# Attention over inducing points, then a gated layer: the first batch's prologue rewritten, and the hidden units dealt out in another order

## The chip, the cores and the metric

One core of a Trainium2 chip runs the whole program. Its engines work side by side and are tied by semaphores: TensorE (PE in the profile, its weight loads PEld), VectorE (DVE), ScalarE (ACT), GpSimd (POOL) and SyncE (SP), which here only issues DMAs. The metric is the device time of one execution in microseconds; a smaller one is better.

## The reference, cut to what matters

```python
# x: (4, 12416, 128), inducing: (32, 128); w_gate, w_val: (128, 1536), w_out: (1536, 128)
def mab(q, kv):                                   # scale = 1/sqrt(128)
    s = scale * (q @ kv.transpose(0, 2, 1))
    s = s - s.max(-1, keepdims=True)
    a = np.exp(s)
    a /= a.sum(-1, keepdims=True) + 1e-09
    return a @ kv
h = mab(I, x)                                     # 32 inducing rows attend over all 12416 rows
y = mab(x, h)                                     # each row attends over the 32 rows of h
gate = 1 / (1 + np.exp(-(y @ w_gate)))
return gate * (y @ w_val) @ w_out
```

So a batch's `h` needs every row of that batch before the first row of output can be made. The kernel never forms `y`: it multiplies `h` into the two weight matrices once per batch (`hw`, 32 rows by 2 x 1536 columns) and applies the attention weights `a2` to that.

## The kernel before, in words

**Groups and stages.** A batch is 97 chunks of 128 rows: six groups of 16 chunks and one odd chunk. *Stage 1* (`s1_...`) takes a group's scores against the inducing rows, their maximum per 32-partition strip, the exponentials, and the weighted sum of the rows. *Combine* rescales the seven group sums to one maximum, adds them and gives `hT` (`h_take`). `hw_fill` multiplies `hT` into the weights: four matmuls per half, two from `wg16` and two from `wv16`, each of 32 x 384 outputs into its own strip of 32 partitions; a ScalarE copy brings the half into the tile `hwt`. *Stage 2* (`s2_...`) gives each chunk's weights `a2` over the 32 rows of `h`, four times side by side (`s2_spread`), transposed so that they can be multiplied with `hwt`.

**The main loop.** 97 blocks of four chunks go through 12 slices of 128 hidden units each, taken two and one at a time: `steps`, 776 of them. For step t, `hidden_mm` makes the gate (`g_ps`) and the value (`v_ps`) from `hwt` and `a2`; `gate` is ScalarE's tanh of the gate (sigmoid by tanh, line 830); `product` is VectorE's `(t + 1) * v` into `u` (line 841); `project` multiplies `u` with `wo16` into `acc_ps` (line 870), which ScalarE copies out once per block. The gate fill of step t + 2 follows the value fill of step t, so TensorE's order is value t, gate t + 2, then whatever else is planned there, then projections.

**What sets the order.** The schedule is written by hand: every engine runs its instructions in the order of the Python calls. `plan` maps a slot (two steps, about 1.7 us apart) to the pieces of the next batch's stage 1, combine and stage 2 that are issued there; `part` (an `hw_fill` half) and `keep` (its copy) are such pieces, two of each for each of three later batches. A wait in front of an instruction holds everything behind it on the same engine.

**The prologue** (batch 0) has no main loop to hide behind. POOL's queue issues the loads: batch 0's six groups, the last in two pieces of 12 and 4 chunks, then the three weight matrices and the first three groups of batch 1. As each group lands, TensorE transposes it (`x_turn`, line 631, into `xt_ps`), VectorE copies the first eight chunks to `xT` and ScalarE the rest. The first three groups in order of arrival (`EARLY` = 3) are combined on GpSimd while later ones still come. For the rest the chain at the end is: maximum of the last group, `ml` over all columns, weights `wl`, four scaled sums added by VectorE; beside it GpSimd and ScalarE find the common maximum over the four strips (`join_min`, lines 352 to 367), whose factor `w4` scales `e32l` and `e32w`; two matmuls (lines 735 and 737) give the sum of weights and `h`. After `hT` the first block of four chunks (`a2n_a`, `a2T`, `a2first`) is done by VectorE and TensorE, the other twelve chunks through two DMA transposes on SP.

**Dummy matmuls.** `keep_on(n, tag)` issues n matmuls of 128 x 512 that nobody reads. Their operand `idle` is the last four chunks of `xT[0]`, so a real copy into those four chunks has to wait until the dummies issued before it have read them.

Of the kernel before, what the change touches and what calls it, by code (L numbers as in the profile page):

```python
# [19 lines left out]
BC = 4  # L20
# [5 lines left out]
def kernel(  # L26
# [73 lines left out]
    def keep_on(n, tag):  # L100
# [33 lines left out]
        wo16[:].rearrange("p j c -> p (j c)"), moe_w_out.rearrange("(p j) c -> p (j c)", j=NJ)  # L134
    )
    for g in range(3):
        x_load(1, g)
# [24 lines left out]
    EARLY = NS - 4  # L162
# [115 lines left out]
    def s1_sum_keep(b, s, hp):  # L278
        ng, w, R = s1_dims(s)
        width = C + 1 if b else C  # L280
        summed[b] += 1
        if b == 0 and at_col[s] > EARLY:
            return hp[:, 0:C]
        nc.scalar.copy(out=hsts[b % 2][0:R, at_col[s], 0:width], in_=hp[0:R, 0:width])
# [51 lines left out]
    def hw_fill(b, hf, tag):  # L336
        hw_ps = ps.tile([P, NI // 2, P], F32, tag=tag, name="hw_ps")
        for r in range(4):
            wsrc = wg16 if r < 2 else wv16
            nc.tensor.matmul(  # L340
                hw_ps[32 * r : 32 * r + 32, :, :],
                hT16[b][:],
                wsrc[:].rearrange("c (f i t) -> c i t f", i=NI, t=2)[:, ts(hf, NI // 2), r % 2, :],
# [3 lines left out]
        return hw_ps  # L347

# [21 lines left out]
    def plan_combine(b, lead, weights, fill):  # L370
# [45 lines left out]
        def keep(hf):  # L416
            if hf == 0:
                st["hwt"] = bp.tile([P, NI, P], F16, tag="hw", bufs=B, name="hwt")
            nc.scalar.copy(out=st["hwt"][:, ts(hf, NI // 2), :], in_=st["hw_ps"][:])  # L419
            if hf == 1:  # L420
                hw[b] = st["hwt"]
# [218 lines left out]
    for p in range(-2, NS - 3):  # L640
# [7 lines left out]
        if p >= 0:  # L648
            s = arrival[p]
            a1[s] = s1_turn_copy(s, s1_turn_pe(0, s, a1T[s]))  # L650
# [3 lines left out]
        if p + 1 == EARLY - 1:  # L654

# [7 lines left out]
            lw = const.tile([P, EARLY], F32, tag="lwe")  # L663
            nc.gpsimd.tensor_tensor(out=lw[:], in0=l1[:, 0:EARLY], in1=we[:], op=ALU.mult)
            add_tree(lw, EARLY, l1l[:, 0:1])
# [12 lines left out]
        elif p == EARLY - 1:  # L678
            pool_part(1)
        elif p == EARLY:  # L680
            pool_part(2)
# [7 lines left out]
    s = arrival[EARLY]  # L689
    s1_sum(0, s, a1[s], "acc")  # L690
    a1T[sb] = s1_exp(0, sb, s1)
    aT = s1_turn_pe(0, sa, a1T[sa])
    a1T[sc] = s1_exp(0, sc, s1_score(0, sc, "g1"))
    keep_on(4, "acc")


    ml = const.tile([P, 1], F32, tag="ml")
    nc.vector.tensor_reduce(out=ml[:], in_=nml[:], axis=AX.X, op=ALU.min)
    wl = const.tile([P, 1 + NS - EARLY], F32, tag="wl")
    nc.scalar.activation(out=wl[:], in_=nml[:], func=AF.Exp, bias=ml[:], scale=-1.0)  # L700
    nc.scalar.mul(out=hpart[0][:], in_=hpart[0][:], mul=wl[:, 0:1])
    a1[sa] = s1_turn_copy(sa, aT)
    a1[sb] = s1_turn_copy(sb, s1_turn_pe(0, sb, a1T[sb], "g2"))
    hps = [hst[:, EARLY, 0:C], s1_sum(0, sa, a1[sa], "acc")]
    lw = const.tile([P, 1 + NS - EARLY], F32, tag="lwl")
    nc.vector.tensor_mul(out=lw[:], in0=l1l[:], in1=wl[:])
    lsum = const.tile([P, 1], F32, tag="lsum0")
    nc.vector.reduce_sum(out=lsum[:], in_=lw[:], axis=AX.X)
    e32s = const.tile([P, m], F32, tag="e32s")
    nc.scalar.mul(out=e32s[:], in_=e32[:], mul=lsum[:])  # L710
    top = join_min(const, ml, (1, 3))
    w4 = const.tile([P, 1], F32, tag="w4")
    nc.scalar.activation(out=w4[:], in_=ml[:], func=AF.Exp, bias=top[:], scale=-1.0)
    e32l = const.tile([P, m], F32, tag="e32l0")
    nc.scalar.activation(
        out=e32l[:], in_=e32s[:], func=AF.Identity, bias=tiny[:], scale=w4[:]
    )
    e32w = const.tile([P, m], F32, tag="e32w")
    nc.scalar.mul(out=e32w[:], in_=e32[:], mul=w4[:])

    a1[sc] = s1_turn_copy(sc, s1_turn_pe(0, sc, a1T[sc], "v2"))
    hps.append(s1_sum(0, sb, a1[sb], "m"))
    hps.append(s1_sum(0, sc, a1[sc], "v1"))
    keep_on(4, "g2")
    for k, hp in enumerate(hps):
        nc.vector.scalar_tensor_tensor(
            out=hpart[0][:],
            in0=hp,
            scalar=wl[:, 1 + k : 2 + k],
            in1=hpart[0][:],  # L730
            op0=ALU.mult,
            op1=ALU.add,
        )
    l_ps = ps.tile([P, m], F32, tag="g1", name="l_ps")
    nc.tensor.matmul(l_ps[:], ones[:], e32l[:], start=True, stop=True)
    h_ps = ps.tile([P, m], F32, tag="m", name="h_ps")
    nc.tensor.matmul(h_ps[:], hpart[0][:], e32w[:], start=True, stop=True)
    keep_on(2, "g2")
# [19 lines left out]
    s2_score(0, NLO + BC, 0, GC - BC, s2_b)  # L758
    hl_b = s2_max(GC - BC, s2_b)
    hw[0] = bp.tile([P, NI, P], F16, tag="hw", bufs=B, name="hwt")  # L760
    hw_ps = [hw_fill(0, 0, "g1"), hw_fill(0, 1, "v1")]
    keep_on(2, "g2")
    for hf in range(2):
        nc.scalar.copy(out=hw[0][:, ts(hf, NI // 2), :], in_=hw_ps[hf][:])
# [5 lines left out]
    e_b = s2_exp(GC - BC, s2_b, *hl_b)  # L770
    a2T = ps.tile([P, BC, P], F16, tag="m", name="a2T_ps")
    for j in range(BC):
        nc.tensor.transpose(
            a2T[:, j, :],
            a2n_a[2 * j // BC][:, j % (BC // 2), :, :].rearrange("p r k -> p (r k)"),
            ident[:],
        )
    a2first = s2p.tile([P, BC, P], F16, tag="a2first", bufs=1)
    keep_on(1, "g2")
    nc.vector.tensor_copy(out=a2first[:], in_=a2T[:])  # L780
# [203 lines left out]
```

## Time and profile before

| | us |
|---|---|
| Median of three runs (lowest, highest) | 729.85 (728.44, 729.98) |
| The profiled execution's own time | 727.66 |
| Its span, first to last instruction | 725.8 |
| Busy in that span: VectorE, ScalarE, TensorE, GpSimd | 706.7, 676.7, 648.4, 419.4 |
| Start of the first product (line 841) in the span | 32.26 |

The profiled execution is one of the same program under the hardware profiler; 1.9 us of its time lie outside the span. Lines of the timeline read: start, duration, engine, line, operation, out<-in, how many are merged (`x4`), and in brackets the idle time before it and who ended it. Lines of the windows read: stretch, its length, busy time of the engine and in brackets its number of instructions, granted TensorE clock, share of the DMA engines, GB/s.

### The profile page before, as it was taken

The page shows a single profiled execution, that of the slowest core. Times are in us where ns is not written, and L with a number is a line of the kernel's source. Part 1 is how long each engine was busy: PE and PEld are TensorE (multiplying, and loading weights), DVE is VectorE, ACT ScalarE, POOL GpSimd, SP SyncE. Part 2 cuts the span into 40 slices and gives each one's busy share as a digit, 9 for nine tenths or more (in the row PEclk, how much of TensorE's full clock was granted, in tenths as well). Part 3 has the DMA queues.
Part 4 walks back from the last instruction along what each step waited for, and adds up shares of the span by engine and source line. Part 5 has one row for each costly group of instructions (what it writes and reads, how often), then busy time and mean ns, then how long its engine had stood idle before and what let it go on. Part 6 is the DMA issues. An engine that isn't in the chain of part 4 may idle for free.

```text
span 725.8 us, 21496 instructions
## 1 busy us (share of the span) xinstructions
PE 648.4 (89%) x8437; PEld 390.4 (54%) x8437; DVE 706.7 (97%) x874; ACT 676.7 (93%) x1011; POOL 419.4 (58%) x702
## 2 busy tenths in 40 slices
PE   7888899999998998999989988999899899898887
PEld 4455555555555555555555555555555555555555
DVE  4899999999999999999999999999999999999998
ACT  4799999999999999999999999999999999999996
POOL 4463754887654648488666266387755665636200
PEclk9999999999999999999999999999999999999999
DMA  9999635242459253235248431220223122131311
GB/s 173 174 188 159 126 81 117 63 101 72 92 117 170 73 113 87 62 79 114 59 119 160 104 75 53 67 75 30 76 59 67 52 60 71 46 62 45 61 45 46
DMA packets 116342, 65.21 MB, mean 90 GB/s; under 512 B 99824, under 2 KB 100496, under 8 KB 116240
## 3 DMA queue, kind: packets, MB, share of 16 engines
q1 hardware_dynamic: 111936, 49.81, 30.1%
q0 software_dynamic: 4032, 13.90, 10.7%
q8 instruction: 66, 1.08, 0.6%
q14 instruction: 36, 0.29, 0.1%
q10 hardware_dynamic: 272, 0.13, 0.1%
HBM read 27.80 MB, written 25.43 MB: 73 GB/s over the span
## 4 chain that ended last, share of the span: by engine, by line
DVE 50%; issue 21%; PE 17%; ACT 9%; DMA 2%; DVEq 1%; POOL 0%; ACTq 0%; POOLq 0%
DVE u L841 47%; ACT t L830 8%; PE acc_ps L870 8%; PE v_ps L812 6%; DMA xn<-in_x_dram 2%; DVE nm L221 2%; PE hw_ps L340 1%; DVEq L841 1%; ACT a1T L234 1%; PE g_ps L812 0%; PE hp_ps L269 0%; POOL xn L81 0%; ACT hwt L419 0%; PE w_ps L103 0%; PE s_ps L437 0%
## 5 line engine op out<-in xcount | busy, mean ns | idle before, releaser
L841 DVE SCALAR_TENSOR_TENSOR u<-t,v_ps 128x1024 f16<-128x1024 f16 (+1 forms) x777 | 675.6, 944 | 3.1 <-PE g_ps L812 2.9
L830 ACT ACTIVATE t<-g_ps 128x1024 f16<-128x1024 f32 (+1 forms) x776 | 594.0, 818 | 28.7 <-ACT t L830 17.3
L812 PE MATMUL v_ps<-a2r,hwt 32*128 32x512 f16 (+1 forms) x1188 | 292.4, 371 | 65.9 <-DVE u L841 64.2
L870 PE MATMUL acc_ps<-wo,u 128*128 128x128 f16 x4656 | 327.3, 220 | 1.0
L870 PEld LDWEIGHTS <-u 128*128 128x128 f16 x4656 | 261.6, 98 | 89.3 <-issue 87.4
L812 PE MATMUL g_ps<-a2r,hwt 32*128 32x512 f16 (+1 forms) x1188 | 295.4, 377 | 0.0
L812 PEld LDWEIGHTS <-hwt 32*128 32x128 f16 x2400 | 90.5, 91 | 199.4 <-issue 153.3
L506 POOL TENSOR_TENSOR sum<-e 128x256 f32<-128x256 f16 (+1 forms) x23 | 15.5, 672 | 144.5 <-ACT e L498 142.5
L552 POOL TENSOR_TENSOR a2n<-e,rs 128x2048 f16<-128x2048 f16 (+2 forms) x24 | 86.3, 3594 | 6.8 <-DVE rs L524 5.1
L530 POOL TENSOR_TENSOR near<-sme,minus 128x16 f32<-128x16 f32 (+1 forms) x22 | 65.2, 2966 | 1.8
L888 ACT ACTIVATE o<-acc_ps 128x512 f32<-128x512 f32 x96 | 58.0, 605 | 0.9
L485 POOL TENSOR_SCALAR rise<-rise 128x256 f32<-128x256 f32 (+6 forms) x110 | 51.2, 466 | 9.7
L484 POOL TENSOR_TENSOR rise<-sc 128x256 f32<-128x256 f32 (+1 forms) x22 | 16.3, 739 | 40.1 <-ACT sc L474 39.8
L486 POOL TENSOR_TENSOR top<-top,rise 128x128 f32<-128x128 f32 (+3 forms) x88 | 28.4, 323 | 7.3
L506 POOL TENSOR_TENSOR sum<-sum 128x128 f32<-128x128 f32 (+3 forms) x92 | 28.4, 309 | 7.2
L484 POOL TENSOR_TENSOR rise<-top 128x128 f32<-128x128 f32 (+3 forms) x88 | 27.3, 311 | 6.9
L489 POOL TENSOR_TENSOR sc<-sc,top 128x512 f32<-128x512 f32 (+1 forms) x22 | 23.9, 1086 | 1.7
L437 PEld LDWEIGHTS <-xT 128*128 128x128 f16 x388 | 13.1, 96 | 11.8 <-issue 11.7
L81 POOL DMA_DIRECT2D xn<-in_x_dram x25 | 14.7, 596 | 6.6 <-DMA xn<-in_x_dram 5.7
L437 PE MATMUL s_ps<-hT,xT 128*128 128x32 f16 x388 | 18.1, 178 | 0.1
L486 POOL TENSOR_TENSOR top<-sc,rise 128x256 f32<-128x256 f32 (+1 forms) x22 | 16.2, 738 | 1.8
L234 ACT ACTIVATE a1T<-s_ps,nm 128x512 f16<-128x512 f32 (+1 forms) x24 | 15.0, 626 | 1.7 <-DVE nm L221 1.7
(121 smaller groups left out, 245.1 us busy)
## 6 DMA issues: line engine op xcount, KB each, us to landing
out_dram<-o SPq DMA_DIRECT2D x96, 256.0 KB, 2.1
xn<-in_x_dram POOLq DMA_DIRECT2D x19, 512.0 KB, 7.2
xn<-in_x_dram POOLq DMA_DIRECT2D x4, 544.0 KB, 5.9
a2r<-a2n SPq DMA_TRANSPOSE x29, 4.4
xn<-in_x_dram POOLq DMA_DIRECT2D x1, 384.0 KB, 14.7
wg<-in_moe_w_gate_dram POOLq DMA_DIRECT2D x1, 384.0 KB, 16.2
wv<-in_moe_w_val_dram POOLq DMA_DIRECT2D x1, 384.0 KB, 16.4
wo<-in_moe_w_out_dram POOLq DMA_DIRECT2D x1, 384.0 KB, 15.7
```

The lines of the kernel that those rows point to most:

```text
L437: nc.tensor.matmul(s2[:, j, :], xT[b][:, c + j, :], hT16[b][:], start=(j == 0), stop=whole and j == j1 - 1, skip_group_check=True,)
L484: nc.gpsimd.tensor_tensor(out=r, in0=far, in1=near, op=ALU.subtract)
L485: nc.gpsimd.tensor_scalar_max(out=r, in0=r, scalar1=0.0)
L486: nc.gpsimd.tensor_tensor(out=top[:, 0:n, 0:w], in0=near, in1=r, op=ALU.add)
L506: nc.gpsimd.tensor_tensor(out=d[:, 0:n, :], in0=src[:, :, 0:w], in1=src[:, :, w : 2 * w], op=ALU.add)
L530: nc.gpsimd.tensor_tensor(out=near[:, 0:n], in0=sme[:, 0:n], in1=minus1[:, 0:n], op=ALU.pow)
L552: eng.tensor_tensor(out=a2n[:, 0:n, :, :], in0=e.unsqueeze(2).to_broadcast((P, n, 4, m)), in1=rs.unsqueeze(2).unsqueeze(3).to_broadcast((P ...
L812: st[what + "end"] = nc.tensor.matmul(pt[:, k, col : col + nb * P], hw[b][r : r + 32, j // 2, :], a2r[r : r + 32, o : o + nb, :].rearrange ...
L830: st["tanh"] = nc.scalar.activation(out=st["t"][:], in_=st["g"][:], func=AF.Tanh, scale=0.5)
L841: u = nc.vector.scalar_tensor_tensor(out=st["u"][:, :, c:e], in0=st["t"][:, :, c:e], scalar=1.0, in1=st["v"][:, :, c:e], op0=ALU.add, op1= ...
L870: nc.tensor.matmul(acc[0][(i // 2) % len(acc[0])][:, i, :], st["u"][:, k, ts(i, P)], wo16[:, j, :], start=(j == 0 and i in ((0, 2) if len( ...
L888: nc.scalar.mul(out=o32[:], in_=acc[0][0][:], mul=0.5)
```

## The change

The hidden units are dealt out in another order. Before, slice j = 2i + t of `hwt` took the columns f * 12 + j of the weights, so a fill read every twelfth column; now a fill reads 384 columns that lie side by side, and the copy out of PSUM (`hw_take`) picks every third value instead. `wo16` is loaded in the matching order, in four pieces per partition instead of one.

In the prologue: `EARLY` is 4; the sum of the fourth group is finished behind the loop; the last group's transposes are split 8, 4 and 4, with the copy of the middle four on ScalarE; the maximum over the four strips is found by TensorE (`mlT_ps`: `ml` turned into a row; a reduction; four small matmuls that subtract it into `arg_ps`), so that one exponential gives the final `wl`; the four scaled sums are added by TensorE in PSUM; `join_min` is no longer called for batch 0. The first block's weights are not spread: 16 transposes write the four strips. The other twelve chunks' `a2n_b` goes from VectorE to GpSimd and behind the first half of the first product (`turn_b`). The first step's gate fill, tanh and product are cut in halves. Batch 1's third group is loaded later, and some of batch 1's slots move by one to three.

```diff
-        wo16[:].rearrange("p j c -> p (j c)"), moe_w_out.rearrange("(p j) c -> p (j c)", j=NJ)
+        wo16[:].rearrange("p (q i) c -> p q (i c)", i=NI // 2),
+        moe_w_out.rearrange("(q p i) c -> p q (i c)", p=P, i=NI // 2),
...
-    EARLY = NS - 4
+    EARLY = NS - 3
...
     def hw_fill(b, hf, tag):
...
-                wsrc[:].rearrange("c (f i t) -> c i t f", i=NI, t=2)[:, ts(hf, NI // 2), r % 2, :],
+                wsrc[:, ts(2 * (r % 2) + hf, F // 4)],
...
+    def hw_take(hwt, hf, hw_ps):
+        nc.scalar.copy(
+            out=hwt[:, ts(hf, NI // 2), :], in_=hw_ps[:].rearrange("r (f i) -> r i f", i=NI // 2)
+        )
...
-    x_turn(0, c0, GC - BC, "g2")
     s1 = s1_score_pe(0, sb, "v1")
-    x_turn(0, c0 + GC - BC, BC, "v2")
     s1_max(0, sb, s1)
...
+    x_turn(0, c0, GC // 2, "g2")
+    xt = ps.tile([P, 2, 8, P], F16, tag="v2", name="xt_ps")
+    for j in range(GC // 2):
+        nc.tensor.transpose(xt[:, j // BC, j % BC, :], xn[0][:, c0 + GC // 2 + j, :], ident[:])
+        if j == BC - 1:
+            two = nc.scalar.copy(
+                out=xT[0][:, c0 + GC // 2 : c0 + n - BC, :], in_=xt[:, 0, 0:BC, :]
+            )
+    keep_on(2, "acc")
+    one = nc.vector.tensor_copy(out=xT[0][:, c0 + n - BC : c0 + n, :], in_=xt[:, 1, 0:BC, :])
...
+    nc.tensor.matmul(mlT_ps, ml[:], identf[:], start=True, stop=True)
+    nc.tensor.matmul(arg_ps, identf[:], nml[:], start=True, stop=True, skip_group_check=True)
...
+    for g in range(4):
+        nc.tensor.matmul(
+            low_ps[32 * g : 32 * g + 32, 1, 0:NL],
+            top[:],
+            ones[0:1, 0:NL],
...
+    nc.scalar.activation(out=wl[:], in_=arg_ps, func=AF.Exp, scale=-1.0)
...
+    nc.gpsimd.tensor_tensor(out=lw[:], in0=l1l[:], in1=wl[:], op=ALU.mult)
+    add_tree(lw, NL)
...
-    top = join_min(const, ml, (1, 3))
...
+        nc.tensor.matmul(h_ps[:], hw_parts[k], e32[:], start=(k == 0), stop=(k == NL - 1))
...
-    a2n_a = [
-        s2_spread(BC // 2, e_a[:, j : j + BC // 2, :], rs_a[:, j : j + BC // 2], nc.vector)
-        for j in range(0, BC, BC // 2)
-    ]
...
     for j in range(BC):
...
+        for r in range(4):
+            nc.tensor.transpose(a2T[32 * r : 32 * r + 32, j, :], a2n_a[:, j, :], ident[:])
...
+            cuts = [0, 512] if t else [0, 256, 512]
...
+            if t == 0 and c == 0:
+                turn_b()
...
-            [(11, (18, 19, 19)), (16, (23, 23, 23))]
+            [(13, (18, 19, 19)), (16, (23, 23, 23))]
...
-            when = 3 * g if b else (7, 10, 13, 16, 19, 22, 11)[g]
+            when = 3 * g if b else (9, 11, 14, 17, 20, 23, 12)[g]
```

Where instructions move: three places. Rows name line, operation, out<-in, shape, and in brackets the engines or DMA queues (DMASW) whose semaphores are waited for.

TensorE, at the last group's transposes (`xt_ps`), the dummies (`w_ps`) and the last group's scores (`s_ps`). Before:

```order
L209 MATMUL s_ps<-xT_87,indT 32x512 [waits Activation_49]
L209 MATMUL s_ps<-xT_87,indT 32x512
...
L631 MATMUL xt_ps<-ident,xn_92 128x128 [waits PE_49]
...
L269 MATMUL hp_ps<-xn_92,a_358 32x128 [waits Activation_49]
...
L209 MATMUL s_ps<-xT_87,indT 32x512 [waits DVE_49]
...
L103 MATMUL w_ps<-xT_87 128x512 [waits Activation_49]
```

Now:

```order
L637 LDWEIGHTS xn_92 [waits DMASW5_49]
...
L695 MATMUL xt_ps<-ident,xn_92 128x128 [waits PE_49]
...
L695 LDWEIGHTS xn_92 [waits DMASW6_49]
L695 MATMUL xt_ps<-ident,xn_92 128x128 [waits Activation_49]
...
L103 MATMUL w_ps<-xT_87 128x512 [waits PE_49]
...
L210 MATMUL s_ps<-xT_87,indT 32x512 [waits DVE_49]
...
L270 LDWEIGHTS a_409 [waits DVE_49]
```

The last four transposes now wait for ScalarE, whose copy reads the same PSUM tile; two dummies follow them, and the copy of the last four chunks on VectorE (line 701) stands behind those dummies. The weighted sum of the fourth group (`a_409`) has moved behind the last scores.

GpSimd, between the early groups' sums (`hpart`) and stage 2 of the first group (`hi`). Before:

```order
L673 TENSOR_TENSOR hpart_284<-hpart_284,hpart_285 128x128 [waits Pool_49]
L352 COPY quad<-ml 32x1 [waits DVE_49]
L352 COPY quad<-ml 32x1 [waits Pool_49]
...
L353 TENSOR_SCALAR quad<-quad 32x1 [waits Pool_49]
L361 TENSOR_SCALAR quad<-quad 32x1 [waits Pool_49]
L367 COPY top<-quad 32x1 [waits Pool_49]
...
L452 CAST hi<-nmx 128x12 [waits DVE_49,Pool_49]
```

Now:

```order
L680 TENSOR_TENSOR hpart_320<-hpart_320,hpart_321 128x128 [waits Pool_49]
L748 TENSOR_TENSOR lw<-l1l,wl 128x4 [waits Activation_49]
L325 TENSOR_TENSOR lw<-lw 128x2 [waits Pool_49]
L325 TENSOR_TENSOR lw<-lw 128x1 [waits Pool_49]
L751 TENSOR_SCALAR e32l<-e_124,lw 128x32 [waits Pool_49]
L458 CAST hi<-nmx 128x12 [waits DVE_49]
```

`join_min` is gone; in its place stand four operations that start only when ScalarE has made `wl`, each waiting for the one before, and `e32l` is what the sum of weights (`l_ps`) needs.

TensorE, at the first step. Before:

```order
L812 MATMUL g_ps<-a2first,hwt 128x512 [waits PE_49]
L812 MATMUL g_ps<-a2first,hwt 128x512
...
L812 MATMUL v_ps<-a2first,hwt 128x512
...
L103 MATMUL w_ps<-xT_87 128x512 [waits Activation_49]
```

Now:

```order
L103 MATMUL w_ps<-xT_87 128x512 [waits PE_49]
...
L853 MATMUL g_ps<-a2first,hwt 128x256 [waits PE_49]
...
L853 MATMUL g_ps<-a2first,hwt 128x256
...
L853 MATMUL g_ps<-a2first,hwt 128x256 [waits DVE_49]
...
L853 MATMUL g_ps<-a2first,hwt 128x512
...
L853 MATMUL v_ps<-a2first,hwt 128x512
```

The two gate matmuls of step 0 have become four half ones, the second pair waiting for VectorE's second half of `a2first`. The first tanh half waits for the fourth of them, not the second; the second tanh half has no wait of its own.

More of the change, by code (lines that the diff above doesn't have):

```diff
@@ L418, in keep @@
                 st["hwt"] = bp.tile([P, NI, P], F16, tag="hw", bufs=B, name="hwt")
[L419 removed]
+            hw_take(st["hwt"], hf, st["hw_ps"])
             if hf == 1:
@@ L690 @@
+    keep_on(2, "acc")
+    one = nc.vector.tensor_copy(out=xT[0][:, c0 + n - BC : c0 + n, :], in_=xt[:, 1, 0:BC, :])
+    tc.declare_no_dep(one.ins, two.ins, reason="each reads a bank of its own")
+    a1T[sb] = s1_exp(0, sb, s1)
+    s = arrival[EARLY - 1]
+    a1[s] = s1_turn_copy(s, aT)
+    s1 = s1_score_pe(0, sc, "g1")
+    s1_max(0, sc, s1)
     s1_sum(0, s, a1[s], "acc")
-    a1T[sb] = s1_exp(0, sb, s1)
-    aT = s1_turn_pe(0, sa, a1T[sa])
-    a1T[sc] = s1_exp(0, sc, s1_score(0, sc, "g1"))
@@ new lines @@
+    a1[sb] = s1_turn_copy(sb, aT)
+    hps = [s1_sum(0, sa, a1[sa], "acc")]
+    for g in range(4):
[3 more added lines that the diff above has]
+            ones[0:1, 0:NL],
+            start=False,
+            stop=True,
+            skip_group_check=True,
+        )
+    aT = s1_turn_pe(0, sc, a1T[sc], "v1")
+    wl = const.tile([P, NL], F32, tag="wl")
+    nc.scalar.activation(out=wl[:], in_=arg_ps, func=AF.Exp, scale=-1.0)
+    hw_parts = [hpart[0][:]] + [hst[:, NS - k, 0:C] for k in range(1, NL)]
@@ L735 @@
+    h_add(0)
+    h_add(1)
     nc.tensor.matmul(l_ps[:], ones[:], e32l[:], start=True, stop=True)
-    h_ps = ps.tile([P, m], F32, tag="m", name="h_ps")
-    nc.tensor.matmul(h_ps[:], hpart[0][:], e32w[:], start=True, stop=True)
-    keep_on(2, "g2")
+    h_add(2)
+    h_add(3)
     h_take(0, h_ps[:], l_inverse(l_ps[:]))
@@ L758 @@
     s2_score(0, NLO + BC, 0, GC - BC, s2_b)
+    hw[0] = bp.tile([P, NI, P], F16, tag="hw", bufs=B, name="hwt")
+    for hf, tag in enumerate(("g1", "v1")):
+        hw_take(hw[0], hf, hw_fill(0, hf, tag))
+    keep_on(2, "g2")
     hl_b = s2_max(GC - BC, s2_b)
[L760 to L764, printed above, removed]
```

163 lines of the change are left out of this document (86 added, 77 removed).

## The prediction

> **What bounds the kernel.** I read the page's groups first, then VectorE's waits from the first product to the end, then VectorE's busy time in stretches of 50 us, then the timeline where that falls short, and last the chain through the prologue.
>
> ```profile
> span 725.8 us, 21496 instructions
> L841 DVE SCALAR_TENSOR_TENSOR u<-t,v_ps 128x1024 f16<-128x1024 f16 (+1 forms) x777 | 675.6, 944 | 3.1 <-PE g_ps L812 2.9
> ```
>
> The products alone are 675.6 of 725.8 us, with 3.1 us of idle time before them. So the time is the prologue, plus VectorE's own work, which this change leaves alone but for two small moves, plus that waiting. Where is the waiting?
>
> ```profile
> DVE u L841 <- PE g_ps L812: 2.9, 8, 0.4
> ...
> 150.00:200.00 50.00, 49.27 (x59) 1.00 0.41 92
> 300.00:350.00 50.00, 49.64 (x60) 1.00 0.34 81
> 350.00:400.00 50.00, 49.64 (x59) 1.00 0.61 121
> 500.00:550.00 50.00, 49.27 (x58) 1.00 0.23 60
> ```
>
> Eight waits for TensorE, none above 0.4 us. These four stretches lose 0.73, 0.36, 0.36 and 0.73 us, together 2.18: six waits, two for each later batch. In the timeline the first of them, and a place to compare it with, read:
>
> ```profile
> 163.16 0.83 PE L340 MATMUL hw_ps<-wg,hT 128*32 128x384 f16 x2
> 163.93 0.38 PE L812 MATMUL v_ps<-a2r,hwt 32*128 32x512 f16 x1
> 165.48 2.95 DVE L841 SCALAR_TENSOR_TENSOR u<-t,v_ps 128x1024 f16<-128x1024 f16 x3 [0.36 <-PE g_ps L812]
> ...
> 76.93 0.40 PE L209 MATMUL s_ps<-xT,indT 128*32 128x512 f16 x4
> 77.26 0.38 PE L812 MATMUL v_ps<-a2r,hwt 32*128 32x512 f16 x1
> ```
>
> Half an `hw_fill` (four matmuls of 384 columns; the two on `wg` are shown, those on `wv` run beside them) holds the next value fill for 0.77 us (163.16 to 163.93), and VectorE then goes idle. The last two rows show four matmuls of 512 columns on the same four strips that read in line: 0.33 us (76.93 to 77.26).
>
> The other side of the sum is the prologue:
>
> ```profile
> 4.52 14.70 DMA xn<-in_x_dram
> 26.80 0.20 DVE hT L334
> 32.26 1.09 DVE u L841
> 33.40 0.59 DVE u L841
> ```
>
> Until 19.22 us the last group's first 12 chunks are in flight, which the change doesn't touch. Then come 7.8 us to the end of `hT` (27.00) and 5.26 to the first product, all serial.
>
> **The fills in line: minus 2.18 us.** 384 columns in line take no more than those 0.33 us, so each half frees at least 0.77 - 0.33 = 0.44 us of TensorE, more than the 0.36 that VectorE waits. I take all six waits away: 2.18. Bounds: 0 if something else ends last at the same places; 2.9 if the two waits early in batch 0 go too.
>
> The copy `hw_take` now reads PSUM in steps of three values. The trace has no such read. Bounds: the old 0.48 us, and that times the slowdown of TensorE's strided read, 0.77/384 against 0.33/512 us per column, 3.1-fold: 1.5 us. I take 0.48, the row of the same copy on the same engine. It is covered up to a point:
>
> ```profile
> 168.64 0.48 ACT L419 CAST hwt<-hw_ps 128x384 f16<-128x384 f32 x1
> 169.00 1.54 ACT L830 ACTIVATE t<-g_ps 128x1024 f16<-128x1024 f32 x2
> 170.67 1.21 DVE L841 SCALAR_TENSOR_TENSOR u<-t,v_ps 128x1024 f16<-128x1024 f16 x1
> 31.21 1.03 ACT t L830
> ```
>
> The tanh behind the copy ends at 169.00 + 1.03 = 170.03 and its product starts at 170.67: the copy may take 0.6 us longer before VectorE waits. [...]
>
> **The prologue up to the last maximum: plus 0.7 us.**
>
> ```profile
> 19.96 0.26 ACT L284 COPY hst<-hp_ps 128x128 f32<-128x128 f32 x1
> 20.15 0.59 ACT L635 COPY xT<-xt_ps 128x512 f16<-128x512 f16 x1
> 20.37 0.40 PE L631 MATMUL xt_ps<-ident,xn 128*128 128x128 f16 x4
> 29.00 0.60 PE L103 MATMUL w_ps<-xT 128*128 128x512 f16 x2
> 30.21 0.42 DVE L780 COPY a2first<-a2T_ps 128x512 f16<-128x512 f16 x1 [0.38 <-PE a2T_ps L773]
> 21.15 1.41 DVE L221 TENSOR_REDUCE nml<-s_ps 128x1 f32<-128x512 f32 x2
> ```
>
> Before, the maximum ends at 22.56. Now the last four transposes wait for ScalarE's copy of the middle four, which waits for the `hst` copy (ends 20.22): 20.22 + 0.59 = 20.81. Transposes and then two dummies: the dummies start about 0.25 later (an estimate: what four transposes of 0.40 occupy without their drain) and take 0.60, until 21.66; VectorE's copy of the last four chunks must wait for them, since they read those chunks, plus 0.42: 22.08. The last score matmul 0.40, the maximum 0.70: 23.18, and some 0.1 of hops between engines: 23.3, or +0.7. Bounds: -0.2 if those two waits cost nothing (VectorE is then the limit), +0.9.
>
> **From there to `hT`: minus 0.2.**
>
> ```profile
> 23.33 0.29 ACT L700 ACTIVATE wl<-nml,ml 128x5 f32<-128x5 f32 x1
> 25.92 0.38 PE L735 MATMUL l_ps<-e32l,ones 128*128 128x32 f32 x2
> 26.14 0.39 PE L737 MATMUL h_ps<-e32w,hpart 128*128 128x32 f32 x2
> 17.75 0.21 POOL L664 TENSOR_TENSOR lw<-l,we 128x3 f32<-128x3 f32 x1
> 18.03 0.20 POOL L324 TENSOR_TENSOR lw<-lw 128x1 f32<-128x1 f32 x1
> 26.34 0.36 DVE L329 RECIPROCAL li<-l_ps 128x32 f32<-128x32 f32 x1 [0.37 <-PE l_ps L735]
> ```
>
> Before: 27.00 - 22.56 = 4.44. Now: `ml` 0.2 with its hop; two FP32 matmuls as the pair of lines 735 and 737, 25.92 to 26.53, 0.61; the reduction to `top` 0.25 (an estimate, below the reciprocal's 0.36); four tiny FP32 matmuls, between 0.2 and that pair's 0.61, I take 0.45; `wl` 0.29; four GpSimd operations in a chain at 0.28 each (17.75 to 18.03) 1.12; `l_ps` 0.38; reciprocal 0.36 with 0.1 of hop as now, `hT` 0.20; six more hops of 0.04. Sum 4.2: minus 0.2, so `hT` ends at 27.5. The four scaled sums run beside the GpSimd chain and end before it. Bounds: minus 0.7 to plus 0.3, for the FP32 matmuls that no row shows.
>
> **From `hT` to the second product: minus 0.3.**
>
> ```profile
> 13.32 0.41 PE L269 MATMUL hp_ps<-xn,a 128*32 128x128 f16 x16
> 29.07 0.76 DVE L552 TENSOR_TENSOR a2n<-e_a,rs 128x256 f16<-128x256 f16 x2
> 55.37 0.60 ACT t L830
> 31.73 2.31 POOL L552 TENSOR_TENSOR a2n<-e,rs 128x1024 f16<-128x1024 f16 x1 [2.68 <-DVE rs L524]
> a2r<-a2n SPq DMA_TRANSPOSE x1, 2.6
> ```
>
> Unspread, 128 values per partition instead of 512: 0.76 becomes about 0.29 (an estimate, between half of one of the two and one): -0.47. The 16 transposes have the shape of the 16 matmuls of line 269, 0.41 and a hop, where before the copy starts 0.38 after `a2n` (30.21 - 29.83): +0.07. The copy in halves, 0.28 each by 0.42 for the whole: +0.14, because the first tanh half waits for all four half fills. Half-length fills: -0.1. Tanh of 512 values per partition, 0.60 for 1.03: -0.43. The first product starts 0.79 earlier after `hT`. But it is two halves with a reciprocal between (0.59 + 0.2 + 0.59 against 1.14; 0.2 for 12 columns is an estimate, below the 0.36 of the one with 32), and the second product's value fill stands on TensorE behind the gate fill of step 2, which waits for the second tanh half, 0.52 after the first: 0.79 - 0.52 = 0.27 gained there. `a2n_b` on GpSimd takes half of the 2.31 us of the row with twice its size, 1.2; with the reciprocal 0.8 after the start of the first product and 2.6 for the DMA transpose it lands 4.6 after that start. Block 1's first fill is issued with step 6, three pairs of 1.14 + 0.59 later, 5.2: hidden by 0.6; without that cover it would stop TensorE by what is lacking.
>
> **Sum.** +0.7 - 0.2 - 0.27 - 2.18 = -1.95 us against the profiled execution's 727.66: 725.7. That execution lies 2.19 under the median, so the forecast is 729.85 - 1.95 = **727.9**. The new order of `wo16` leaves its matmuls as they are, and its load is needed only at the first projection, behind the second product. Ten dummies before `hT` become two; the granted clock, 1.00 in every stretch shown, could fall for it, but no row prices that, and I put it in the range alone.
>
> **Rivals.**
>
> - *The prologue is not late* (0.17): the two waits at the last transposes cost nothing, bound -0.2 instead of +0.7. For it: ScalarE's copy could run under VectorE's own queue. Against it: the order of the instructions. 727.9 - 0.9 = 727.0.
> - *A new wait eats part of it* (0.18): batch 1's first group must be transposed before its scores, which move two slots, from 53.60 (their maximum) by 3.5 us to 57.1.
>
> ```profile
> 48.77 3.00 SPq L563 DMA_TRANSPOSE a2r<-a2n  x1
> 53.60 0.68 DVE L221 TENSOR_REDUCE nm<-s_ps 128x1 f32<-128x512 f32 x1
> xT<-xn SPq DMA_TRANSPOSE x21, 4.5
> ```
>
>   Its DMA now stands behind the one at 48.77 and an output: 51.8 + 0.6 + 4.5 = 56.9, just in time for matmuls at 56.7. If TensorE waits there, everything behind does, by up to 1 us, once: 728.9, within the noise.
> - *The strided copies decide* (0.11): slower. At 3.1-fold each takes 1.0 longer, 0.4 beyond its cover, six times 2.4; in the prologue two of them lie in line ahead of the first tanh, 0.9. 727.9 + 3.3 = 731.2. It decides from about 2.3-fold (0.6 us longer), and from 3.2-fold the kernel is slower by more than 0.2%. For it: a read of this kind is what makes the fills slow. Against it: the slow reader there is TensorE, at 0.33 us for what ScalarE takes 0.48 for, so ScalarE asks for fewer values per unit of time.
>
> **How the numbers follow.** The forecast has 0.54. What a measurement of this kernel can tell from no change is about 0.2%, 1.46 us; the forecast lies 0.5 beyond that. Of its 0.54 I put 0.41 on faster and 0.13 within; of the first rival all on faster; of the second 0.02 faster and 0.16 within; of the third 0.02 within and 0.09 slower. Sum: 0.60 faster, 0.31 within, 0.09 slower. Range: the forecast with its bounds reaches from 726.2 (both waits of batch 0 gone too, a prologue 0.9 better) to 729.0; the second rival and half of the third stretch it to 730.2.
>
> **What would show it.** Right: fills of line 341 at about 0.33 us and no idle time before the products near 163, 177, 334, 348, 506 and 520; the first tanh half and first product near 31.9, the second product near 33.4 to 33.7, so a prologue as long as now. Wrong: VectorE idle at the same six places for another reason; the last maximum ending near 22.3; copies of `hwt` above 1.1 us; an idle gap near 57.

## The result and the profile after

The change measured 726.97 us (median of 15 executions, 725.34 to 728.65) against 728.59 for the kernel before (15 executions, one of them 996.96 us long, which the ratio leaves out): ratio 0.9976, 95% interval 0.9964 to 0.9987, so 0.24% faster. The forecast was 727.9 with a range of 726.2 to 730.2; it started from 729.85, a median of three executions that lies 1.26 above that of the fifteen. The other executions of either kernel spread over about 3 us, and the profiled execution of the change, 728.19 us, is one of the longer ones, while that of the kernel before, 727.66, was one of the shortest; so the two spans, 726.4 and 725.8, stand the other way round, and what made the one long has to be found before the profiles can be compared.

From the page of the changed kernel, its group of products; from VectorE's waits between 37 us and the end, the one line that names a product:

```profile
L886 DVE SCALAR_TENSOR_TENSOR u<-t,v_ps 128x512 f16<-128x512 f16 (+1 forms) x778 | 675.6, 945 | 1.8 <-PE g_ps L853 0.9
...
DVE u L886 <- PE g_ps L853: 0.7, 2, 0.4
```

Eight waits of 2.9 us became two of 0.7. VectorE's busy time in the four stretches shown of the kernel before (stretch, length, VectorE busy, granted clock, share and rate of the DMA engines):

```profile
150.00:200.00 50.00, 50.00 (x60) 1.00 0.47 84
300.00:350.00 50.00, 50.00 (x61) 1.00 0.34 81
350.00:400.00 50.00, 50.00 (x59) 1.00 0.61 115
500.00:550.00 50.00, 50.00 (x59) 1.00 0.26 60
```

They are full now. The groups of instructions, by form, show the fills and the copies out of PSUM (count, busy us, mean ns):

```profile
L351 ACT CAST hwt<-hw_ps 128x384 f16<-128x384 f32 x8 | 3.8, 483 | 0.0
...
L341 PE MATMUL hw_ps<-wg,hT 128*32 128x384 f16 x16 | 2.5, 335 | 0.0
```

A fill of 384 columns takes 335 ns in line, and the copy, now the one that reads in steps of three, 483 ns: what it took before. So the later batches gained. The prologue of this execution lost it again. Its chain (start, duration, what):

```profile
4.00 14.13 DMA xn<-in_x_dram
...
22.73 0.59 ACT xT L697
23.36 0.38 PE xt_ps L695 x4
23.75 0.45 PE w_ps L103 x2
24.22 0.44 DVE xT L701
...
25.11 0.70 DVE nml L222
...
30.03 0.20 DVE hT L335
...
36.22 0.27 DVE u L886
```

The last maximum ends at 25.81, 3.25 us later than before. The two waits that the prediction named are there, link for link: ScalarE's copy, the last transposes, the two dummies, VectorE's copy. But x of the last group but one also arrived at 18.13, 1.4 us later than in the profile before, and TensorE's work behind it is slow. The windows (stretch, length, TensorE busy, granted clock, DMA) say why:

```profile
17.50:20.00 2.50, 1.83 (x23) 0.83 1.12 210
20.00:22.50 2.50, 2.50 (x36) 0.50 1.07 205
22.50:25.00 2.50, 1.64 (x12) 0.99 1.30 219
```

TensorE had waited 1.96 us for that x, then ran at half clock for about 3.4 us: at half for 0.85 us of the first stretch shown (0.17 lost of 2.5, doubled), all of the second, 0.05 of the third. The last output copy of VectorE starts at 722.94 here and started at 722.32 before. The stages, from the chains and VectorE's last rows (fills alone, prologue alone and best are experiments below; of the five executions only that of the change was disturbed in this way):

| | before | after | fills alone | prologue alone | best |
|---|---|---|---|---|---|
| last maximum ends | 22.56 | 25.81 | 22.64 | 23.27 | 22.18 |
| from there to the end of hT | 4.44 | 4.42 | 4.44 | 4.42 | 4.51 |
| from there to the second product | 6.40 | 5.99 | 6.39 | 6.43 | 5.99 |
| from there to VectorE's last copy | 688.92 | 686.72 | 686.09 | 689.65 | 686.28 |

### The profile page after: what moved, and what is told of

It reads as the page before. It is cut to its first block, busy times and chain, and to the rows that moved or that the text cites. A ratio compares the mean times of both kernels' runs of the same rounds, so it can differ in the third digit from the quotient of the medians.

```text
span 726.4 us, 21535 instructions
## 1 busy us (share of the span) xinstructions
PE 647.0 (89%) x8461; PEld 391.5 (54%) x8461; DVE 704.7 (97%) x870; ACT 673.9 (93%) x1007; POOL 419.6 (58%) x702
## 3 DMA queue, kind: packets, MB, share of 16 engines
q8 instruction: 66, 1.08, 0.7%
## 4 chain that ended last, share of the span: by engine, by line
DVE 50%; issue 20%; PE 15%; ACT 10%; DMA 3%; DVEq 1%; POOL 0%; SPq 0%; ACTq 0%; POOLq 0%
DVE u L886 48%; ACT t L873 9%; PE acc_ps L917 7%; PE v_ps L853 6%; DMA xn<-in_x_dram 2%; DVE nm L222 1%; DVEq L886 1%; DMA xT<-xn 1%; PE hp_ps L270 1%; PE g_ps L853 1%; PE s_ps L210 0%; POOL xn L81 0%; PE xt_ps L637 0%; ACT a1T L235 0%; ACT hwt L351 0%
## 5 line engine op out<-in xcount | busy, mean ns | idle before, releaser
L886 DVE SCALAR_TENSOR_TENSOR u<-t,v_ps 128x512 f16<-128x512 f16 (+1 forms) x778 | 675.6, 945 | 1.8 <-PE g_ps L853 0.9
L873 ACT ACTIVATE t<-g_ps 128x512 f16<-128x512 f32 (+1 forms) x777 | 594.0, 818 | 28.8 <-ACT t L873 16.9
L558 POOL TENSOR_TENSOR a2n<-e,rs 128x2048 f16<-128x2048 f16 (+3 forms) x25 | 86.8, 3474 | 5.3 <-DVE rs L530 2.4
```

The source lines that it names most:

```text
L558: eng.tensor_tensor(out=a2n[:, 0:n, :, :], in0=e.unsqueeze(2).to_broadcast((P, n, 4, m)), in1=rs.unsqueeze(2).unsqueeze(3).to_broadcast((P ...
L873: st["tanh"] = nc.scalar.activation(out=st["t"][:, :, c:e], in_=st["g"][:, :, c:e], func=AF.Tanh, scale=0.5)
L886: u = nc.vector.scalar_tensor_tensor(out=st["u"][:, :, c:e], in0=st["t"][:, :, c:e], scalar=1.0, in1=st["v"][:, :, c:e], op0=ALU.add, op1= ...
```

## The experiments

**The fills alone.** The kernel before with F dealt in line.

```diff
-                wsrc[:].rearrange("c (f i t) -> c i t f", i=NI, t=2)[:, ts(hf, NI // 2), r % 2, :],
+                wsrc[:, ts(2 * (r % 2) + hf, F // 4)],
...
-                    wo16[:, j, :],
+                    wo16[:, NI * (j % 2) + j // 2, :],
```

> The kernel before with only F dealt in line (the fills, the copy out of PSUM, the order of the output weights); the prologue is the old one. Theory A (the six waits for the gate fill are all the fills cost): 2.2 us under the kernel before, 726.4 against its 728.6, the six idle places near 163 to 523 gone, first product at 32.3 as before. Rival B (the waits go but their time is lost elsewhere in the later batches): within 0.5 us of the kernel before. If A holds, the new prologue gives nothing, since the whole change measured 727.0.

Measured: 725.82 us against 728.42, ratio 0.9967 (0.9955 to 0.9980). Theory A holds and rival B falls. By its median the part is faster than the whole change, but the two intervals overlap (0.9964 to 0.9987 there); the stages decide. Its second product in the chain and its last copy in the timeline, and that last copy in the kernel before:

```profile
33.47 0.59 DVE u L847
...
719.56 0.42 DVE L889 TENSOR_SCALAR o<-acc_ps 128x256 f32<-128x256 f32 x1 [0.38 <-PE acc_ps L876]
```

```profile
722.32 0.42 DVE L883 TENSOR_SCALAR o<-acc_ps 128x256 f32<-128x256 f32 x1 [0.38 <-PE acc_ps L870]
```

From the second product (33.40 before, 33.47 here) to that copy: 688.92 against 686.09, so 2.83 us saved where 2.18 was forecast. Setting the ends of all 777 products of both profiles side by side, the difference jumps at six places and hardly anywhere else:

```
product ending at (us, before)   166.7  181.0  338.1  352.4  509.5  523.8
gained there (us)                 0.46   0.46   0.45   0.45   0.45   0.46
```

That is 2.73; three steps of 0.03 next to them make the rest, to rounding. Each wait cost 0.46, not the 0.36 that its row shows. The group line of the products explains the difference: 777 records of 944 ns are 733.5 us, but their line counts 675.6 us busy, so consecutive records overlap by 0.075 us on average. A product that has to wait starts after the end of the one before, and loses that overlap on top of the idle time shown. By undisturbed stages the part saves 2.76 us up to the last copy (722.32 to 719.56), the whole change 1.92 (the sum behind the point-by-point account).

**The prologue alone.** The changed kernel with F dealt as before.

```diff
-                wsrc[:, ts(2 * (r % 2) + hf, F // 4)],
+                wsrc[:].rearrange("c (f i t) -> c i t f", i=NI, t=2)[:, ts(hf, NI // 2), r % 2, :],
...
-                    wo16[:, NI * (j % 2) + j // 2, :],
+                    wo16[:, j, :],
```

> The changed kernel with F dealt as before (strided fills, plain copy, old order of the output weights): only the new prologue and first step are left. Theory A (the sum of the prediction: +0.7 -0.2 -0.27): 0.2 us over the kernel before, 728.8, and the six idle places back. Rival C (this prologue loses TensorE's clock after its long wait near 16 to 18 us more often than the old one): 729.5 to 730.5, with granted clock near 0.997 in most executions. Rival D (the new prologue gains what it was built for): 727.6 or less.

Measured: 729.85 us against 728.42, ratio 1.0019 (1.0009 to 1.0029), so the new prologue by itself makes the kernel slower. The median lies in rival C's range, but the clock that this rival asks for in most executions shows in half of them (0.998 in 6 of 12); theory A's 728.8 is passed by 1 us. Its profiled execution had x at 16.71 and full clock, and is the clean copy of the chain above:

```profile
4.00 12.71 DMA xn<-in_x_dram
...
20.18 0.59 ACT xT L694
...
21.20 0.45 PE w_ps L103 x2
21.67 0.44 DVE xT L698
...
22.57 0.70 DVE nml L221
...
27.49 0.20 DVE hT L334
...
34.12 0.27 DVE u L883
```

Every time of the prediction's chain is met within 0.1: copy to 20.77 (said 20.81), dummies to 21.65 (21.66), VectorE's copy to 22.11 (22.08), maximum to 23.27 (23.3). It is 0.71 later than before. So is the second product (34.12 against 33.40, 0.72), since the new first step gains nothing here, and from there to the last copy another 0.73 us go (689.65 against 688.92), 0.44 of which is the late transfer that the run with the slot alone shows below. That is why theory A's 0.2 fell short.

**Without the two waits.** All eight transposes of the last half go first, and the dummies read other chunks.

```diff
-        if j == BC - 1:
-            two = nc.scalar.copy(
-                out=xT[0][:, c0 + GC // 2 : c0 + n - BC, :], in_=xt[:, 0, 0:BC, :]
-            )
-    keep_on(2, "acc")
+    two = nc.scalar.copy(out=xT[0][:, c0 + GC // 2 : c0 + n - BC, :], in_=xt[:, 0, 0:BC, :])
+    keep_on(2, "acc", xT[0][:, 0:4, :])
```

> The changed kernel with the two waits at the last transposes taken away: all eight transposes of the last half are issued ahead of ScalarE's copy, and the two dummies read chunks of x that are long in place. Theory A (those waits are on the path): 0.7 us under the changed kernel, 726.3, with the last maximum ending 0.7 sooner behind the last transpose. Rival E (the path there is VectorE's own queue or the arrival of x): 726.9 to 727.1.

Measured: 726.75 us (724.52 to 727.64) against 726.97 for the change (725.34 to 728.65); ratio to before 0.9974 (0.9964 to 0.9985). The medians alone tell nothing, because the executions of both spread over 3 us; the ends of the two spreads are 0.8 and 1.0 apart. The profile tells more (windows of TensorE as above, then the chain):

```profile
20.00:22.50 2.50, 2.50 (x42) 1.00 1.07 203
```

```profile
23.02 0.70 DVE nml L222
```

The x of the last group but one landed at 18.29 and the maximum ended at 23.72, 5.43 us later. In the prologue alone, at full clock too, it was 6.56 (16.71 to 23.27). The two dummies still stand at their place here, so the 1.1 us between the two are the waits: theory A's mechanism, with more than its 0.7. The clock stayed at 1.00 although TensorE had waited 2.04 us for that x, longer than in the change.

**Three more dummies in the long wait.**

```diff
         if p + 2 < NS - 1:
+            if p == NS - 4:
+                keep_on(3, "v2")
             x_turn(0, *groups[arrival[p + 2]], ("g2", "v2")[p % 2])
```

> The changed kernel with three more dummies on TensorE ahead of the transposes of the last group but one, where it waits longest for x (1.96 us in the profile of the change, and the clock was 0.50 for the 3.4 us behind it). Rival C (the fall of the clock is what makes the new prologue long): the granted clock stays 0.999 to 1.000, the time falls by 0.5 to 1.5 us to 725.5 to 726.5, and the runs lie closer together. Theory A (the clock does not decide): 727.0, or 0.1 more where x lands early and the dummies are still running.

Measured: 729.66 us, ratio to before 1.0019 (1.0008 to 1.0031): a miss in the sum, 2.7 us over the change's median, and the granted clock, which rival C wanted at 0.999 or more, was 0.998 or less in all eight executions. Up to the maximum the dummies did what they were for: with x at 17.88, 0.25 earlier than in the change, the clock stayed at 1.00 and the maximum (first row, from the chain) ended at 24.38 instead of 25.81. But the clock fell all the same, 10 us later than in the change, from 29.15 to 32.56 (windows of TensorE, last fence), and from hT to the second product it took 6.72 us instead of 5.99. The larger loss is near 60 us (the transfer in this run's chain and in that of the change, then windows of VectorE's busy time):

```profile
23.68 0.70 DVE nml L222
...
53.87 6.17 DMA xT<-xn
```

```profile
54.60 4.87 DMA xT<-xn
```

```profile
58.00:60.00 2.00, 1.22 (x2) 0.97 1.07 103
60.00:62.00 2.00, 1.25 (x2) 0.50 0.79 176
62.00:64.00 2.00, 0.81 (x2) 0.50 0.77 193
64.00:66.00 2.00, 1.46 (x3) 0.50 1.07 200
66.00:68.00 2.00, 1.93 (x3) 0.83 0.33 66
```

```profile
30.00:32.50 2.50, 2.50 (x25) 0.50 0.02 3
```

This is the place of the second rival: batch 1's first group, whose scores the change moved to slot 13. Its DMA transpose took 6.17 us, TensorE waited 2.14 for it (in the profile of the change 0.86), the clock fell to half, and 3.3 us of VectorE's time went: 10 us less the 6.67 that the windows show as busy.

**The first step alone,** on top of the fills: first block unspread, first step in halves, the rest of the block normalized by GpSimd.

```diff
-    a2n_a = [
-        s2_spread(BC // 2, e_a[:, j : j + BC // 2, :], rs_a[:, j : j + BC // 2], nc.vector)
-        for j in range(0, BC, BC // 2)
-    ]
+    a2n_a = s2p.tile([P, BC, m], F16, tag="a2n_a", bufs=1)
...
+        for r in range(4):
+            nc.tensor.transpose(a2T[32 * r : 32 * r + 32, j, :], a2n_a[:, j, :], ident[:])
...
-        cuts = [0, 512] if t < NST - 1 else [0, 256, 512]
+        cuts = [0, 512] if 0 < t < NST - 1 else [0, 256, 512]
```

> The kernel before with F dealt in line and, of the prologue's parts, only the new first step (first block unspread, first step in halves, the rest of the block normalized by GpSimd); the way to hT and batch 1's slots are the old ones. The prediction gave this step -0.27 us. Theory A2 (read from the second set of profiles: hT to the end of the second product took 7.09 us before and 7.13 with the new step): within 0.1 us of the fills alone, 725.8. Prediction's theory: 725.5, with the second product 0.27 sooner behind hT. Rival F (its DMA transposes or the longer code shift the loading of code onto a transfer): 727 or more.

Measured: 725.88 us, ratio 0.9969 (0.9959 to 0.9980), the same as the fills alone (0.9967) within the spread. Its chain:

```profile
28.89 0.20 DVE hT L335
...
35.07 0.26 DVE u L860
```

From hT's end (29.09) to the second product 5.98 us, 0.41 less than with the fills alone (27.08 to 33.47): the prediction's direction and a little more than its 0.27, and theory A2, which had read no gain from the run with the old fills, falls. There the fills of 0.86 us keep TensorE, and the two matmuls behind them stand in front of the new transposes (timeline of the prologue alone: start, duration, idle time before):

```profile
29.75 0.29 DVE L796 TENSOR_TENSOR a2n_a<-e_a,rs 128x128 f16<-128x128 f16 x1
...
30.29 0.33 PE L464 MATMUL s_ps<-lo,identb 128*128 128x384 bf16 x1
...
31.00 0.49 DVE L809 COPY a2first<-a2T_ps 128x256 f16<-128x256 f16 x2 [0.96 <-PE a2T_ps L805]
```

The weights are ready at 30.04, their copy starts 0.96 later; in the changed kernel 0.5 later. So this part needs the fills in line to gain anything. Behind the second product this kernel falls 0.49 us back against the fills alone, in six steps of 0.02 to 0.17 us between 238 and 571 us, whose cause was not traced; in the profile that eats the gain.

**The dummies moved,** from the last transposes to the long wait (the edit of the run without the two waits, with `keep_on(2, "v2")` where the three stood).

> The changed kernel with the eight transposes of the last half issued together and the two dummies moved from there to TensorE's long wait for x two groups earlier, so the number of instructions on TensorE stays that of the change. Theory A (the two waits cost 0.7): 726.3 and the last maximum ending near 22.6 where x lands at 16.7. Theory C (the clock's fall behind that wait costs about 2 us where it happens): granted clock 0.999 or more in most executions, and with the 0.7 then 725.5 to 726.0. If the kernel with three more dummies was slow only because its code loaded 1.2 us earlier onto batch 1's first DMA transpose, this one, with the count unchanged, does not show the 1.2 to 1.5 us gaps near 60.

**And batch 1's first transfer one slot earlier.**

```diff
-            when = 3 * g if b else (9, 11, 14, 17, 20, 23, 12)[g]
+            when = 3 * g if b else (8, 11, 14, 17, 20, 23, 12)[g]
```

> As the run before it, and batch 1's first DMA transpose is issued one slot (1.73 us) earlier. Theory G (TensorE waits near 58 for that transfer, 0.14 us of VectorE's idle time, more where a load of code falls on it): the idle time near 58 to 59 is gone, 0.15 us less than the run before it, and no execution with a long stop there. Rival: the DMA queue in front of it is the limit (it stands behind an output and another transpose), so the transfer lands as late as now: no difference.

> The kernel with moved dummies and the earlier transfer once more, on the same chip as the two others of this set, since its first set had five executions: 724.4 to 724.9 if that median holds, with granted clock 0.999 or more in most executions; 725.3 or more if it was luck.

Measured: moved dummies 725.27 us, ratio 0.9963 (0.9950 to 0.9975), below both theories' figures, and no idle time above 0.15 us near 60 in its profile. Here too, and in the first run of the next kernel, the clock fell later in the prologue instead, at 28.8 and 28.9. With the slot 724.36, ratio 0.9952 (0.9940 to 0.9964), and again 724.39, ratio 0.9953 (0.9940 to 0.9966). That is the lowest median of the study, 2.6 us under that of the change; by the ratios, each to the kernel before measured beside it, 0.24% or 1.7 us (0.9952 against 0.9976). The chain of its second run, where x landed early (16.70), and the start of its last output copy in the timeline:

```profile
20.04 0.61 DVE xT L639
...
21.48 0.70 DVE nml L222
...
26.49 0.20 DVE hT L335
...
32.68 0.27 DVE u L884
...
718.96 0.42 DVE L928 TENSOR_SCALAR o<-acc_ps 128x256 f32<-128x256 f32 x1 [0.38 <-PE acc_ps L915]
```

VectorE's own queue is the limit before the maximum now, which ends at 22.18: 1.09 sooner than in the prologue alone with the same arrival of x. Its first run had x at 17.87, like the run with three dummies (17.88), and full clock up to the maximum as that one had; the maximum ended at 23.30 against 24.38:

```profile
22.60 0.70 DVE nml L222
```

Two pairs, 1.09 and 1.08, and the 1.13 of the run without the two waits, whose dummies had not moved: the waits cost 1.1 us. Without them the new prologue would have been 0.4 ahead of the old one at this point.

**The old kernel without eight of its ten dummies.**

```diff
-    keep_on(4, "acc")
...
-    keep_on(4, "g2")
```

> The kernel before with eight of the ten dummies ahead of hT taken away, as the change has it. Theory C (they kept the clock up): the clock falls to half for 3.4 us in more executions, 0.998 or less, median 729.5 to 730. Rival H (the dummies stand in the way of nothing and hold nothing): 728.4 as before. Rival I (they were on the path, which the chain of waits of the kernel before puts at 5.6% of its shown stretch): 727.7 to 728.1.

Measured: 729.17 us against 727.95, ratio 1.0016 (1.0007 to 1.0025). Theory C holds in its sign, though the median lies under its 729.5 to 730: the granted clock was 0.998 or less in all 11 executions, where the kernel before had that in 5 of 26 on the same chip. TensorE's busy time and clock:

```profile
25.00:27.50 2.50, 1.52 (x6) 0.70 1.07 218
27.50:30.00 2.50, 2.50 (x27) 0.62 1.06 211
```

By these rows the fall begins near 26.0 (0.30 lost of the first stretch, doubled, is 1.5 us at half), right behind the place of the second four.

**The slot alone,** in the changed kernel (the one edit on `when` above).

> The changed kernel with one edit: batch 1's first DMA transpose is issued one slot (1.73 us) earlier. Theory G (that transfer is late for the scores that the change moved to slot 13: products lose 0.24 us near 58 to 63 in the profile of the change, and win 0.18 there in the run with the earlier transfer): 0.4 us under the changed kernel, 726.6 where that measured 727.0, with no idle time of VectorE at 59 to 62. Rival (the 0.9 us between the two runs with moved dummies came from their clock, not from the slot): no difference, 727.0.

Measured: 725.53 us (725.23 to 730.96), ratio to before 0.9978 (0.9963 to 0.9994). Seven of 12 executions at full clock lie at 725.2 to 725.7, the others above 727, so the median owes part of its 1.4 us to the clock; by the ratios (0.9976 for the change) nothing is gained at all. The profile is plainer; second product and last copy:

```profile
36.12 0.27 DVE u L886
...
722.40 0.42 DVE L930 TENSOR_SCALAR o<-acc_ps 128x256 f32<-128x256 f32 x1 [0.38 <-PE acc_ps L917]
```

686.28 us between them against 686.72 in the change: the late transfer costs 0.44, as theory G said. The other profiles bear it out: with the late transfer this stage took 686.69 to 686.72 (the change, without the two waits, dummies moved), with the earlier one 686.23 to 686.30 (four kernels or runs). Of the kernels with the whole change only the one with three dummies, 689.99, stands apart.

**The transposes of the first block set first,** in the best kernel.

```diff
-    e_b = s2_exp(GC - BC, s2_b, *hl_b)
     a2n_a = s2p.tile([P, BC, m], F16, tag="a2n_a", bufs=1)
...
     keep_on(1, "g2")
+    e_b = s2_exp(GC - BC, s2_b, *hl_b)
```

> The best kernel so far (dummies moved, transfer one slot earlier) with the 16 transposes of the first block set ahead of the two matmuls that finish the scores of the rest of the block. Theory J (the transposes stand behind those two in TensorE's queue): 0.2 to 0.3 us less than that kernel, 724.1, most where the clock is at half there; the first tanh starts sooner behind hT than 3.75 us. Rival: at full clock those two matmuls are done before the weights to transpose are ready, and their exp now comes later in ScalarE's queue, ahead of the first tanh: no difference or 0.2 more.

Measured: 725.87 us, ratio 0.9974 (0.9961 to 0.9987). Theory J falls, the rival holds: at full clock the second product starts 6.13 us after hT (28.01 to 34.14) instead of 5.99. That is 0.14 slower; the rest of the 1.5 us in the median goes with a lower clock, which was 0.997 or less in 6 of 12 executions.

## Why the prediction was right, point by point

It was right in its mechanisms but one, and in its sum by luck: the terms were off in both directions, -0.65 and -0.14 against +0.18 and +0.63, and the misses cancel to 0.03.

- *The fills, minus 2.18.* Right mechanism, term too small: 2.83 measured. The step "more than the 0.36 that VectorE waits. I take all six waits away" priced a wait by its idle time alone; each also cost about 0.1 of lost overlap, 0.46 in all. The upper bound 2.9 was set for another reason (two more waits gone, which stayed) and held by luck.
- *The prologue up to the last maximum, plus 0.7.* Met: 0.71 in the undisturbed profile, link by link. The first rival, that the waits cost nothing, falls.
- *From the maximum to hT, minus 0.2.* Wrong by the whole term: 4.42 against 4.44. The failing step is "The four scaled sums run beside the GpSimd chain and end before it". The chain of the change, and GpSimd's last operation:

```profile
28.34 0.41 PE hp_ps L270 x16
28.75 0.56 PE h_ps L762 x4
29.31 0.22 PE l_ps L768 x2
29.53 0.46 PE h_ps L762 x4
```

```profile
28.65 0.29 POOL L751 TENSOR_SCALAR e32l<-e,lw 128x32 f32<-128x32 f32 x1
```

  GpSimd is done at 28.94. The last group's own sum, `hp_ps`, ends on TensorE at 28.75, and eight FP32 matmul records for `h_ps` with two for `l_ps` among them follow in that engine's order, to 29.99. The sums end last. The GpSimd chain itself came about when the sum had it, 3.13 us after the maximum.
- *From hT to the second product, minus 0.27.* Right mechanism, 0.41 measured, but only together with the fills in line; with the old fills it gained nothing (6.43 against 6.40), which the prediction did not say.
- *The second rival, a new wait near 57.* It was given 0.18 as an alternative to the forecast; it happened beside it. It cost 0.44, within the "up to 1 us", in the change's own profile, and 3.3 us where the transfer was 1.3 us longer.
- *Not in the sum:* a further 0.19 us net between the second product and the end (686.28 with the slot mended, 686.09 with the fills alone); the losses in it are three steps of 0.08 to 0.18 near 240 and 335 us, cause not traced.
- *The third rival, slow strided copies,* falls: 483 ns against the old 0.48 us.
- *The clock.* "The granted clock, 1.00 in every stretch shown, could fall for it, but no row prices that": it fell. In the change 11 of 15 executions had 0.998 or less; in the kernel before 7 of 26, 5 of 26 and 2 of 23 in the three later sets. Its price in one comparison of two profiles with late x: from x to the maximum 7.68 us in the change (18.13 to 25.81), 6.50 with the clock held (17.88 to 24.38), so 1.2 us. Taking the dummies out of the old kernel raised its median by 1.2.

The undisturbed sum is +0.71 - 0.02 - 0.41 - 2.83 + 0.63 (the slot's 0.44 and the 0.19) = -1.92, beside the -1.95 forecast. The measured medians are 1.62 apart, and the forecast's start from 729.85 added 1.26 to its absolute figure. The profiled execution came out 0.62 behind the old one (722.94 against 722.32), since late x and the clock together added 25.81 - 23.27 = 2.54.

*The range.* Its 726.2 and, ahead of the rivals, its 729.0 do not follow from the stated bounds: with the bounds of the first three terms it would run from 725.8 (0.72, 0.9 and 0.5 under the forecast) to 730.8 (2.18, 0.2 and 0.5 over it). The measured time lies inside either way.

Late x: in 8 of the 13 profiles the last group but one landed at 17.9 to 18.3, in 5 at 16.7. Late were seven of the nine profiles with the new prologue and one of the four with the old; so few do not tell whether the new prologue makes it likelier. The best kernel had one of each. In each of the 13 a 16 KB packet of the instruction queue ran near 16 us, early arrivals included; whether it bears on the time at which x lands was not tried.

## What to carry to other kernels

Price a wait on a saturated engine by its idle time plus the overlap that its neighbours' records show (records times mean, less the busy time), not by the idle time alone: here 0.46 us for each wait of 0.36. When a prologue is reordered, look at what each dummy reads and at which tile two copies share: here the waits so made cost 1.1 us, and moving two dummies to where TensorE was idle anyway made the change 1.7 us faster by the ratios, together with one transfer issued a slot earlier. Where dummies are taken out, test them alone: the eight removed here were worth 1.2 us in the old kernel.

## What was not expected of the hardware

- In the change the granted clock fell at 19.14, after a gap on TensorE of 1.96 us (16.21 to 18.17), and stayed at 0.50 for 3.41 us, though TensorE was busy for all of the 2.50 us from 20.00 to 22.50. In the old kernel with fewer dummies it fell near 26.0, with TensorE busy for 1.87 us from 22.5 to 25.0 and for 0.02 from 25.0 to 26.0.
- The gap alone does not decide: after 2.04 us (16.30 to 18.34, the run without the two waits) the clock stayed at 1.00, and in the three profiles where it fell at 28.8 to 29.2 TensorE was busy for 86% of the 3.41 us ahead. But four falls begin a whole multiple of 3.413 us, the length of the change's fall in its trace, after the trace first shows the clock at 1.00: 4 of them in the change (5.49 to 19.14), 6 in the old kernel with fewer dummies (5.50 to 25.98), 7 and 16 with three dummies (5.26 to 29.15 and 59.87). What in TensorE's work brings on a fall was not tested.
- Three dummies and their weight loads were followed, 40 us later, by a DMA transpose of 6.17 instead of 4.87 us. A packet of the instruction queue ran at 58.0, inside that transfer, while in the change it ran at 60.3, behind it. Of the first two DMA transposes of batch 1 in the 13 profiles, those with such a packet in their flight landed 3.07 to 3.69 us after SyncE's instruction ended (12), those without 1.39 to 2.37 us (14). Counted from the second product, the packet came after 22.5 us in this run and after 23.5 to 24.3 in the others with the new prologue. That added instructions shift such a packet onto a transfer fits this; no run took the shift away alone.
- ScalarE's copy out of PSUM in steps of three FP32 values costs what the copy in line had cost (483 ns against 0.48 us, 128x384), while TensorE's fills in steps out of SBUF had taken more than twice as long as in line (0.83 against 0.34 us).
